# Filling products cut to TensorE's form, a normaliser and key features that read PSUM, and the gate column computed with k and v

## The chip, the cores and the metric

The kernel runs on one core of one Trainium2 chip. A core has five engines with an instruction queue each: TensorE (PE: matrix products from SBUF into PSUM; its weight loads are listed as PEld), VectorE (DVE), ScalarE (ACT), GpSimd (POOL) and SyncE (SP), which here issues all DMAs. Each engine takes its instructions in the order in which they were written; between engines there are semaphores. PSUM has eight banks of 512 float32 columns on 128 partitions.

The metric is the device time of one execution, in microseconds; a change is judged by the median of several runs.

## The reference

Two branches read the same input `x` (2048 positions, 512 features), and a gate mixes them. Branch A is attention with 32 heads of 16 dimensions and one shared key and value head; branch B is a gated MLP whose second half is mixed over the positions.

```python
g = _sigmoid((x * gate_w).sum(-1, keepdims=True))
# A: 32 heads share k and v
q = (x @ wq).reshape(B, S, H, Dh); k = x @ wk; v = x @ wv
scores = jnp.einsum('bhqd,bkd->bhqk', q, k) * Dh ** (-0.5)
o = jnp.einsum('bhqk,bkd->bhqd', softmax(scores), v)
a = o.reshape(B, S, H * Dh) @ wo
# B
z = gelu(jnp.einsum('bsd,df->bsf', x, w_in))
z1, z2 = z[..., :Fh], layernorm(z[..., Fh:])
gg = jnp.einsum('ts,bsf->btf', w_sp, z2) + b_sp[None, :, None]
b = jnp.einsum('bsf,fd->bsd', z1 * gg, w_out)
return g * a + (1 - g) * b
```

S = 2048, D = 512, H = 32, Dh = 16, Fh = 688. Arrays are bfloat16; products sum in float32.

## The kernel before

**Attention without scores.** The scores are small, so the kernel takes exp as a polynomial of the third degree. Then numerator and denominator of the softmax are polynomials in q, whose coefficients are sums ("moments") over all keys: products of k's components times v. A guard checks the bound on the scores; where it fails, a general path runs (not taken here).

**Early stage (0 to about 35 us).** `x` is loaded in four quarters and transposed on TensorE (`g_x`). `g_kv(c)` computes k and v of a quarter (L675, 16 small products), VectorE copies v (L679) and k times 0.25 (L682) from PSUM to SBUF, and then VectorE or GpSimd, whichever the planner finds free, forms products of k's components from the SBUF copy: `inside` (L688, five operations; L684 is the helper's line, L689 the last copy), `across` (L693), `phi` (L698) and `rkv` (L701). `moments` sums them over the keys on TensorE, `moments_out` turns the sums into weights T3, T2b, M2 and so on.

**z2, z1, Q.** The MLP's input products and their gelu: `g_z2` (128 x 344, whole array), `g_z1` (five groups of 128 columns and one, `half5`, cut into four strips), and the q projections (`g_q`).

**Units (59 to 274 us).** 16 units, one for 8 heads' worth of rows (`G`) and a quarter of the queries (`tg`): linear forms of q (L818, squared on ScalarE), four "W" products (L849) into banks 0 to 3, which VectorE (L860) and ScalarE plus GpSimd (L864, L865) multiply by copies Y of q, and sums over them (L871 and L867 to L869). Banks 0 to 3 hold one W group or one group of squares at a time.

**The normaliser**, once for each `tg` (`g_den`, L878): four small strip products give the denominators in PSUM; VectorE adds a constant (L885), takes the reciprocal (L886), multiplies by the gate's part `Er` (L887), all in SBUF float32 (`Rf`), and splits the result into a bfloat16 and its remainder (L891, L892, `Rh`). TensorE spreads `Rh` over the rows (L897, "Rr"), VectorE multiplies the numerators by it (L898).

**Filling work.** The mixing over positions (`g_sp`: 17 products for each of 5 whole groups and one strip group, four times), and the output (`g_out`: 4 + 6 products for each of 16 tiles). The weights of the mixing are loaded by transposing DMAs.

**The gate.** A strided DMA puts `gate_w` into column 32 of `wkvg` (L1040); `g_gate` forms x times gate_w along the columns (strip products), `g_gs` the same along the rows (64 products of one column, L772); both go through exp after the last gelu (L779).

**Who sets the order.** A planner (`Plan.run`) simulates the engines with the costs given in `add` and writes each engine's order; the chip keeps that order. A task has a priority (`pri`, lower first). On TensorE a task knows its *form*: whole array, four column strips, two halves of the rows (W), or four quarters of the rows (squares). Where a task's form differs from the one that TensorE stands in, its priority is worse by 2 and 100 ns are charged. In the kernel before, the form of a product is fixed: `mm1` (L593) is whole, `mmq` (L598) and `half5` (L927) are strips. A group of products opens a PSUM bank and closes it when all its readers ("evac") are done.

Of the kernel before, what the change touches and what calls it, by code (L numbers as in the profile page):

```python
# [16 lines left out]
S = 2048  # L17
# [31 lines left out]
SWITCH = 100.0  # L49
# [5 lines left out]
LAZY = 12  # L55

# [237 lines left out]
class Plan:  # L294
# [8 lines left out]
    def add(self, eng, cost, fn, r=(), w=(), pri=50.0, grp=None, evac=False, dma=0, size=0, chan=None, rate=DMA_RATE, tag="", after=(), opens=(), hold=(), slack=0.0, swp=SWITCH_PRI):  # L303
# [6 lines left out]
        t.tiles = getattr(fn, "tiles", 1)  # L310
# [33 lines left out]
    def run(self, prog, allowed):  # L344
# [6 lines left out]
        tiles = 1  # L351
# [43 lines left out]
        while done < len(self.tasks):  # L395
# [25 lines left out]
            for rt, t in cand[e]:  # L421
# [12 lines left out]
                k = (t.pri + (t.swp if e == "pe" and t.tiles != tiles else 0.0), t.idx)  # L434
# [48 lines left out]
def build_kernel(nc, x_d, wq_d, wk_d, wv_d, wo_d, win_d, wsp_d, bsp_d, wout_d, gw_d, out_d):  # L483
    es = ExitStack()
    with es:
# [24 lines left out]
        gwr = sb("gwr", [128, 4, 32], B16)  # L510
        wo = sb("wo", [128, 4, D], B16)
# [31 lines left out]
        Rf = sb("Rf", [128, 2, 128], F32)  # L543
# [51 lines left out]
        def mmq(b, n, off, lhsTs, rhss, start, stop):  # L595

            def f(t):
                return [t.matmul(ps[32 * q:32 * q + 32, 512 * b() + off:512 * b() + off + n], lhsTs[q], rhss[q],  # L598
                                 start=start, stop=stop, tile_position=(0, 32 * q)) for q in range(4)]
            f.tiles = 4  # L600
            return f
# [46 lines left out]
        add("pool", 1600.0, lambda g: g.memset(psi, 0.0), w=[("psi", c) for c in range(4)], pri=-1)  # L648
# [22 lines left out]
        def g_kv(c):  # L671
            g = Group("any")
            for k in range(4):
                for dt in range(4):
                    add("pe", 26.0, mm1(lambda g=g: g.b, 32, 64 * k, xT[:, dt, 512 * c + 128 * k:512 * c + 128 * k + 128], wkvg[:, dt, 0:32], dt == 0, dt == 3),  # L675
                        r=["wk", "wv", ("x", c, dt)], grp=g, pri=0, tag="kv")
# [5 lines left out]
            add("dve", 130.0, lambda v: v.tensor_scalar(kx[:, t4, :], src()[:, :, 0:16], 0.25, None, ALU.mult), w=[("rk", c)], grp=g, evac=True, pri=0, tag="rk")  # L682
            kq = kx[:, t4, :].rearrange("p k (g i) -> p k g i", i=4)
            mul = lambda v, lo, n, a, b, i: v.tensor_tensor(psi[:, t4, lo:lo + n].rearrange("p k (g i) -> p k g i", i=i), a, b, ALU.mult)  # L684

            def inside(v):

                out = [mul(v, 0, 16, kq, kq, 4), mul(v, 16, 12, kq[:, :, :, 0:3], kq[:, :, :, 1:4], 3), mul(v, 28, 8, kq[:, :, :, 0:2], kq[:, :, :, 2:4], 2),  # L688
                       mul(v, 36, 4, kq[:, :, :, 0:1], kq[:, :, :, 3:4], 1), v.tensor_copy(psi[:, t4, 56:64], kx[:, t4, 0:8])]  # L689
# [626 lines left out]
```

## Time and profile before

| | us |
|---|---|
| median of 3 runs | 300.37 (300.25 to 300.68) |
| the profiled execution | 300.82 |
| its span, first to last instruction | 299.0 |

| engine | instructions | larger groups (us) |
|---|---|---|
| TensorE | 2406 products, 2406 weight loads | mixing 87.3, W 39.2, output 26.3 and 17.1, z2 21.1, sums 20.7 |
| VectorE | 313 | L860 81.8 |
| ScalarE | 232 | L864 71.3, L822 31.1 |
| GpSimd | 96 | L865 136.2 |

The mean granted clock of TensorE is 0.984 of full speed. A row of a group of instructions reads: line, engine, operation, output<-inputs, shape, count, then busy time, mean duration in ns, and the idle time of the engine ahead of it with what ended it. A row of the timeline reads: start, length, engine, line, operation, count. On TensorE the numbers ahead of the shape are rows\*columns of the array. A row of the windows reads: stretch, length, then busy time (and count) of TensorE, weight loads, VectorE, ScalarE, GpSimd, then granted clock, DMA share, GB/s. A row of the waits reads: who, at which line, for whom: total us, times, the longest.

### The profile page before, as it was taken

Reading aid. Unit: us, or ns where it says so; the run is one execution under the profiler, and the core shown is the slowest. Engines: PE = TensorE matmul, PEld = TensorE weight load, DVE = VectorE, ACT = ScalarE, POOL = GpSimd, SP = SyncE. Lnnn points to the kernel's source line nnn. Section 1 sums busy time; section 2 is a strip of 40 time slices with the busy share of each in tenths; the row PEclk is TensorE's granted clock in tenths of the full one; section 3 lists DMA queues with packets and bytes.
Section 4 is the critical chain, followed back from the end, with each engine's and each line's share of the span. In section 5 each row is a group of like instructions: output and inputs, shape, how many; then the busy total and the mean of one; then the engine's idle time right before and its main releaser. Section 6 shows DMA issues by size and latency. Waiting matters only on the chain.

```text
span 299.0 us, 6100 instructions
## 1 busy us (share of the span) xinstructions
PE 279.7 (94%) x2406; PEld 116.1 (39%) x2406; DVE 185.3 (62%) x313; ACT 171.8 (57%) x232; POOL 160.3 (54%) x96
## 2 busy tenths in 40 slices
PE   7897999999999999999997999999969999988992
PEld 3575654444443333332341334233334333233440
DVE  1799996073756796464559586634696734797102
ACT  3484887779884645678571646576324467642001
POOL 8673121055758474674955274957470957775200
PEclk9999999999999999999999899999997999999998
DMA  7938774203786969879960505596932063300002
GB/s 185 347 122 210 166 142 99 44 1 106 213 249 112 208 134 187 165 181 174 168 171 8 142 25 152 107 242 172 158 100 80 0 169 100 106 1 0 3 0 75
DMA packets 51530, 37.56 MB, mean 126 GB/s; under 512 B 36548, under 2 KB 47144, under 8 KB 51496
## 3 DMA queue, kind: packets, MB, share of 16 engines
q1 hardware_dynamic: 51496, 37.12, 54.2%
q8 instruction: 20, 0.33, 0.5%
q14 instruction: 14, 0.11, 0.1%
HBM read 24.52 MB, written 4.19 MB: 96 GB/s over the span
## 4 chain that ended last, share of the span: by engine, by line
PE 72%; DVE 15%; DMA 4%; ACT 2%; SPq 2%; issue 2%; POOL 1%; DVEq 0%; POOLq 0%
PE ps L593 50%; PE ps L849 9%; PE ps L598 9%; DVE Pr L860 3%; DMA X<-qe 2%; DVE Rh L892 2%; PE ps L927 2%; DMA wkvg<-in_A_wv_dram 2%; PE ps L818 2%; DVE wT L684 2%; POOL Pr L865 1%; DVE Rf L887 1%; DVE Pr L698 1%; ACT Wt L864 1%; DVE Rh L891 1%
## 5 line engine op out<-in xcount | busy, mean ns | idle before, releaser
L865 POOL TENSOR_TENSOR Pr<-Wt,Y 128x1024 bf16<-128x1024 bf16 x64 | 136.2, 2129 | 93.8 <-ACT Wt L864 76.0
L860 DVE SCALAR_TENSOR_TENSOR Pr<-ps,T1c,Y 128x1024 bf16<-128x1024 f32 x64 | 81.8, 1278 | 64.0 <-PE ps L849 63.6
L864 ACT ACTIVATE Wt<-ps,T1c 128x1024 bf16<-128x1024 f32 x64 | 71.3, 1115 | 59.1 <-PE ps L849 58.9
L593 PE MATMUL ps<-wT,z 128*128 128x512 bf16 x320 | 87.3, 388 | 0.0
L593 PEld LDWEIGHTS ps<-wT,z 128*128 128x128 bf16 x320 | 28.5, 99 | 44.4 <-issue 20.3
L822 ACT ACTIVATE X<-ps 128x1024 bf16<-128x1024 f32 x32 | 31.1, 1022 | 17.6 <-PE ps L818 17.6
L849 PE MATMUL ps<-X,T 64*128 64x512 bf16 x256 | 39.2, 385 | 1.8 <-DVE Pr L860 1.5
L593 PE MATMUL ps<-wout,z 128*128 128x512 bf16 x96 | 26.3, 381 | 0.8 <-DVE z L966 0.8
L966 DVE TENSOR_TENSOR z<-ps,z 128x512 bf16<-128x512 f32 x20 | 13.7, 686 | 18.1 <-PE ps L593 18.0
L593 PE MATMUL ps<-win,xT 128*128 128x344 bf16 x128 | 21.1, 309 | 0.2
L598 PE MATMUL ps<-Pr,cs 128*32 128x512 bf16 x256 | 20.7, 390 | 0.0
L908 ACT ACTIVATE z<-ps 128x344 bf16<-128x344 f32 x32 | 14.2, 461 | 8.9 <-PE ps L593 6.9
L849 PEld LDWEIGHTS ps<-X,T 64*128 64x128 bf16 x256 | 7.3, 94 | 26.7 <-DVE Pr L860 13.7
L593 PE MATMUL ps<-xT,win 128*128 128x512 bf16 x80 | 17.4, 379 | 0.0
L593 PE MATMUL ps<-wo,win 128*128 128x512 bf16 x64 | 17.1, 380 | 0.0
L992 ACT ACTIVATE outsb<-ps,G 128x512 bf16<-128x512 f32 x14 | 9.6, 689 | 13.0 <-PE ps L593 12.6
L593 PE MATMUL ps<-xT,wq 128*128 128x512 bf16 x64 | 17.0, 379 | 0.1
L898 DVE SCALAR_TENSOR_TENSOR win<-Ns,S,ps 128x512 bf16<-128x512 f32 x16 | 11.7, 741 | 8.5 <-PE ps L593 4.5
L873 ACT ACTIVATE Ns<-ps 128x512 f32<-128x512 f32 x16 | 9.5, 596 | 10.7 <-PE ps L598 10.7
L915 POOL TENSOR_TENSOR rstd<-ve,nhalf 128x4 f32<-128x4 f32 x4 | 4.4, 1092 | 18.6 <-DVE ve L914 18.6
L910 DVE BATCH_NORM_STATS2 bst<-z 128x6 f32<-128x344 bf16 x32 | 14.3, 489 | 0.0
L593 PEld LDWEIGHTS ps<-win,xT 128*128 128x128 bf16 x128 | 11.6, 97 | 5.8 <-issue 0.5
(132 smaller groups left out, 298.9 us busy)
## 6 DMA issues: line engine op xcount, KB each, us to landing
Y<-qe SPq DMA_DIRECT2D x32, 512.0 KB, 4.9
wT<-in_A_x_dram SPq DMA_DIRECT2D x4, 512.0 KB, 5.9
qe<-Qt SPq DMA_DIRECT2D x64, 32.0 KB
out_dram<-outsb SPq DMA_DIRECT2D x16, 128.0 KB, 2.4
X<-qe SPq DMA_DIRECT2D x32, 32.0 KB
Pr<-c_third SPq DMA_DIRECT2D x1, 784.0 KB, 7.9
win<-in_B_w_in_dram SPq DMA_DIRECT2D x2, 344.0 KB, 5.5
win<-in_B_w_in_dram SPq DMA_DIRECT2D x1, 688.0 KB, 8.7
```

What stands on the lines that cost most here:

```text
L593: return lambda t: t.matmul(bank(b(), n, off), lhsT, rhs, start=start, stop=stop)
L598: return [t.matmul(ps[32 * q:32 * q + 32, 512 * b() + off:512 * b() + off + n], lhsTs[q], rhss[q], start=start, stop=stop, tile_position=( ...
L822: add("act", 1030.0, lambda a, h=h: a.activation(X[:, ub, 2 * h:2 * h + 2, :], bank(g.b + 2 * h, 1024).rearrange("p (j n) -> p j n", j=2), ...
L849: return [p.matmul(bank(gw.b + 2 * i + e), T3[64 * e:64 * e + 64, t, :], X[64 * e:64 * e + 64, ub, 2 * h + i, :], start=True, stop=True, t ...
L860: add("dve", 1290.0, lambda v, wv=wv, pi=pi, yv=yv, t=t: v.scalar_tensor_tensor(Pr[:, pi, :, :], wv(), T1c[:, t:t + 1], yv, ALU.add, ALU.m ...
L864: add("act", 1040.0, lambda a, wv=wv, wi=wi, t=t: a.activation(Wt[:, wi, :, :], wv(), ACT.Identity, bias=T1c[:, t:t + 1]), r=["T1c"], w=[( ...
L865: add("pool", 2130.0, lambda v, wi=wi, pi=pi, yv=yv: v.tensor_tensor(Pr[:, pi, :, :], Wt[:, wi, :, :], yv, ALU.mult), r=[("Y", yb, h), ("W ...
L898: add("dve", 750.0, lambda v, gr=gr, u=u, G=G: v.scalar_tensor_tensor(OT[:, tg % 2, G, :], Ns[:, u % NNS, :], S0[:, 0:1], bank(gr.b), ALU. ...
L908: add("act", 456.0, lambda a, g=g, h=h: a.activation(z2[:, FH * st + 344 * h:FH * st + 344 * h + 344], bank(g.b, 344), ACT.Gelu_apprx_tanh ...
L910: add("dve", 495.0, lambda v, h=h: v.bn_stats(bst[:, st, h, :], z2[:, FH * st + 344 * h:FH * st + 344 * h + 344]), r=[("z2", st, h)], w=[( ...
L966: add("dve", 690.0, lambda v: v.tensor_tensor(dst, bank(g.b), dst, ALU.mult), w=[("z1", ft, tc)], grp=g, evac=True, pri=3.5, tag="u")
L992: ea = (620.0, lambda a: a.activation(outsb[:, k, :], bank(g.b), ACT.Copy, scale=G1[:, t2:t2 + 1]))
```

## The change

- **Forms as bits.** Whole, strips, halves and quarters become bits. A new kind of product, `mmx`, is FLEX: whole or strips. If TensorE stands whole, it is issued whole; in strips, or in a form of the rows, it is issued as four strip products of 32 columns each. Q, T2b, Rr, z1 (five groups), the mixing with its bias, and the output become `mmx`. The x transposes, k and v, the moments, z2 and the guard's flag stay whole.

```diff
+        def mmx(b, n, off, lhsT, rhs, start, stop):
+            def f(t):
+                raise AssertionError("no cut chosen")
+            whole = mm1(b, n, off, lhsT, rhs, start, stop)
+            f.cut = {WHOLE: whole, COLS: mmq(b, n, off, [lhsT[:, 32 * q:32 * q + 32] for q in range(4)], [rhs] * 4, start, stop)}
+            f.tiles = FLEX
+            return f
...
-                if t.tiles != tiles:
+                if not t.tiles & tiles:
                     cost += SWITCH
-                tiles = t.tiles
+                    tiles = t.tiles if t.tiles != FLEX else COLS
+                elif t.tiles != FLEX:
+                    tiles = t.tiles
+                if t.tiles == FLEX:
+                    fn = fn.cut[tiles]
```

The planner's charge for a change of form goes from 100 to 110 ns.

- **Normaliser.** One fused operation reads the denominators from PSUM and `Er`; its reciprocal is written into free columns of the same PSUM bank, and the split reads it there. `Er` now holds exp of minus the gate's sum, limited on both sides.

```diff
-            R0, R1 = Rf[:, 0, :], Rf[:, 1, :]
-            add("dve", 280.0, lambda v: v.tensor_scalar(R0, bank(g.b, 128), S * C0, None, ALU.add), w=["R0"], grp=g, evac=True, pri=3, tag="R")
-            add("dve", 1100.0, lambda v: v.reciprocal(R1, R0), r=["R0"], w=["R1"], pri=3, tag="R")
-            add("dve", 290.0, lambda v: v.tensor_tensor(R0, R1, Er[:, 128 * tg:128 * tg + 128], ALU.mult), r=["R1", "Er"], w=["R0"], pri=3, tag="R")
+            R0 = lambda rows=slice(0, 128): ps[rows, 512 * g.b + 128:512 * g.b + 256]
+            add("dve", 290.0, lambda v: v.scalar_tensor_tensor(Rf[:], bank(g.b, 128), S * C0, Er[:, 128 * tg:128 * tg + 128], ALU.add, ALU.mult), r=["Er"], w=["R1"], grp=g, evac=True, pri=3, tag="R")
+            add("dve", 950.0, lambda v: v.reciprocal(R0(), Rf[:]), r=["R1"], w=["R0"], grp=g, evac=True, pri=3, tag="R")
...
-                add("dve", 290.0, lambda v, z=z, a=a, b=b: v.tensor_tensor(Rh[b, z, :], R0[a, :], Rh[a, z, :], ALU.subtract), ...
+                add("dve", 220.0, lambda v, z=z, a=a, b=b: v.tensor_tensor(Rh[b, z, :], R0(a), Rh[a, z, :], ALU.subtract), ..., grp=g, evac=True, pri=3, tag="R")
```

- **Key features.** `inside` and `across` are VectorE's always; `phi` is GpSimd's for quarters 0 and 1 and VectorE's for 2 and 3; `rkv` is GpSimd's always. On VectorE one input (k or v) is read from the PSUM bank of `g_kv`, which stays open until then; GpSimd reads SBUF as before. `across` no longer waits for `inside`. The factor 0.25 goes from the copy of k to the weights: a VectorE operation scales `wk` in place when it has landed.

```diff
-            add({"dve": (950.0, inside), "pool": (2300.0, inside)}, 0, None, r=[("rk", c)], w=[("psi", c)], pri=1, tag="psi")
-            add({"dve": (350.0, across), "pool": (800.0, across)}, 0, None, r=[("rk", c), ("psi", c)], w=[("psx", c)], pri=0.5, tag="psi")
+            ev = dict(grp=g, evac=True)
+            add("dve", 950.0, inside, r=[("rk", c)], w=[("psi", c)], pri=1, tag="psi", **ev)
+            add("dve", 350.0, across, r=[("rk", c)], w=[("psx", c)], pri=0.5, tag="psi", **ev)
```

- **Gate column.** `gate_w` is loaded as one row of 1 KB (`gwl`) right behind wv; four products with a single row turn it into column 32 of `wkvg`, and VectorE copies it there. `g_kv` multiplies by 33 columns in place of 32, so the row sums of the gate come with k and v; `g_gs` with its 64 products is gone, and so is the strided load.

```diff
-                    add("pe", 26.0, mm1(lambda g=g: g.b, 32, 64 * k, xT[...], wkvg[:, dt, 0:32], dt == 0, dt == 3),
-                        r=["wk", "wv", ("x", c, dt)], grp=g, pri=0, tag="kv")
+                    add("pe", 26.0, mm1(lambda g=g: g.b, 33, 64 * k, xT[...], wkvg[:, dt, 0:33], dt == 0, dt == 3),
+                        r=["wk", "wv", "gw", ("x", c, dt)], grp=g, pri=0, tag="kv")
+            add("dve", 80.0, lambda v: v.tensor_scalar(gs[:, t4], src()[:, :, 32], E_MAX, None, ALU.min), w=[("gs", c)], grp=g, evac=True, pri=2.9, tag="gate")
...
+        gw4 = Group("any")
+        for dt in range(4):
+            add("pe", 40.0, mm1(lambda: gw4.b, 1, dt, gwl[:, 128 * dt:128 * dt + 128], ones[0:1, 0:1], True, True), r=["gwl", "ones"], grp=gw4, pri=-0.5, tag="gate")
+        add("dve", 80.0, lambda v: v.tensor_copy(wkvg[:, :, 32:33], bank(gw4.b, 4).unsqueeze(2)), w=["gw"], grp=gw4, evac=True, pri=-0.5, tag="gate")
+        add("pool", 300.0, lambda g: g.tensor_copy(gwr[:], wkvg[:, :, 32:33].broadcast_to([128, 4, 32])), r=["gw"], w=["gwr"], pri=12, tag="gate", slack=20000.0)
```

- **Order.** The first quarter of `x` is loaded ahead of the identity, and z1's last quarter of positions gets priority 14.8 in place of 9.8, behind the first W products (10):

```diff
-                    r=["win1", ("win2", 0), ("x", tc, dt)], grp=g, pri=9.8 + 0.01 * ft, tag="z1")
+                    r=["win1", ("win2", 0), ("x", tc, dt)], grp=g, pri=(9.8 if tc < 3 else 14.8) + 0.01 * ft, tag="z1")
```

More of the change, by code (lines that the diff above doesn't have):

```diff
@@ L48 @@
 DMA_ISSUE = 300.0
-SWITCH = 100.0
+SWITCH = 110.0
 YPRI = 2.1
@@ L309, in add @@
         t.users, t.op, t.eng = [], None, None
-        t.tiles = getattr(fn, "tiles", 1)
+        t.tiles = getattr(fn, "tiles", WHOLE)
         r, w = list(r), list(w)
@@ L350, in run @@
         pipe = [0.0]
-        tiles = 1
+        tiles = WHOLE
         busy = {e: 0.0 for e in ENG}
@@ L433, in run @@
                     continue
-                k = (t.pri + (t.swp if e == "pe" and t.tiles != tiles else 0.0), t.idx)
+                k = (t.pri + (t.swp if e == "pe" and not t.tiles & tiles else 0.0), t.idx)
                 if best is None or k < best[0]:
@@ L638, in build_kernel @@
         load("sp", lambda q: q.dma_start(wkvg[:, :, 0:16], wk_d.rearrange("(dt p) d -> p dt d", p=128)), ["wk"], size=16384, pri=0)
+        add("dve", 80.0, lambda v: v.tensor_scalar(wkvg[:, :, 0:16], wkvg[:, :, 0:16], 0.25, None, ALU.mult), r=["wk"], w=["wk"], pri=-1, tag="wk")
         load("sp", lambda q: q.dma_start(wkvg[:, :, 16:32], wv_d.rearrange("(dt p) d -> p dt d", p=128)), ["wv"], size=16384, pri=0)
+        load("sp", lambda q: q.dma_start(gwl[:], gw_d.rearrange("(one n) -> one n", one=1)), ["gwl"], size=1024, pri=0)
         ld_x(1)
@@ new lines, in inside @@
+                if v is nc.gpsimd:
+                    return out + [v.tensor_copy(psi[:, t4, 56:64], kx[:, t4, 0:8])]
+                return out + [v.tensor_copy(psi[:, t4, 56:64], kp()[:, :, 0:8])]
+            def across(v):
+                up, dn = lambda a: a.unsqueeze(3).broadcast_to([128, 4, 4, 4]), lambda a: a.unsqueeze(2).broadcast_to([128, 4, 4, 4])
+                return [mul(v, psi[:, t4, 64 + 16 * h:80 + 16 * h].rearrange("p k (g i) -> p k g i", i=4), up(kx[:, t4, 8 * h:8 * h + 4]), dn(kx[:, t4, 8 * h + 4:8 * h + 8]),
+                            lambda h=h: up(kp()[:, :, 8 * h:8 * h + 4])) for h in range(2)]
@@ L818, in forms @@
                 return [p.matmul(bank(g.b + j), xe[32 * j:32 * j + 32, :], Qt[32 * j:32 * j + 32, s, :], start=True, stop=True, tile_position=(32 * j, 0)) for j in range(4)]
-            forms.tiles = 3
+            forms.tiles = ROWS32
             add("pe", c_mm(512), forms, r=["cs", ("Q", s)], grp=g, pri=9, tag="sq")
@@ L1039, in build_kernel @@
                             g_z1(ft, tc)
-                    load("sp", nonc(lambda q: q.dma_start(wkvg[:, :, 32:33], gw_d.rearrange("(dt p one) -> p dt one", p=128, one=1))), ["gw"], size=16384, pri=20, hold=[yld[0]])
-                    add("dve", 100.0, lambda v: v.tensor_copy(gwr[:], wkvg[:, :, 32:33].broadcast_to([128, 4, 32])), r=["gw"], w=["gwr"], pri=20, tag="gate")
                     for c in range(4):
                         g_gate(c)
-                    for st in range(NST):
-                        g_gs(st)
                     gate_out()
```

79 lines of the change are left out of this document (41 added, 38 removed).

## The prediction

> **What bounds the kernel now.** I read the page first (its busy times and its chain), then the timeline of TensorE, then the tiles of the normaliser.
>
> ```profile
> span 299.0 us, 6100 instructions
> PE 279.7 (94%) x2406; PEld 116.1 (39%) x2406; DVE 185.3 (62%) x313; ACT 171.8 (57%) x232; POOL 160.3 (54%) x96
> PE 72%; DVE 15%; DMA 4%; ACT 2%; SPq 2%; issue 2%; POOL 1%; DVEq 0%; POOLq 0%
> ```
>
> TensorE is busy 94% of the span and is 72% of the chain that ended last; no other engine is above 62%. But its busy time hides the starts: a row's duration overlaps the next. So I take start-to-start steps from its timeline (start, length, operation, number of matmuls).
>
> ```profile
> 151.16 1.03 PE L593 MATMUL ps<-xT,wq 128*128 128x512 bf16 x4
> 152.02 0.38 PE L593 MATMUL ps<-wT,z 128*128 128x512 bf16 x1
> 152.33 0.73 PE L927 MATMUL ps<-wT,z 128*32 128x256 bf16 x20
> 152.99 0.61 PE L849 MATMUL ps<-X,T 64*128 64x512 bf16 x4
> 153.53 0.40 PE L598 MATMUL ps<-Pr,cs 128*32 128x512 bf16 x4
> 153.76 0.40 PE L598 MATMUL ps<-Prd,cs 128*32 128x128 bf16 x16
> 153.98 0.39 PE L598 MATMUL ps<-Pr,cs 128*32 128x512 bf16 x4
> 154.19 0.23 PE L598 MATMUL ps<-Q,cs 128*32 128x128 bf16 x4
> ```
>
> 128\*128 is the whole array, 128\*32 one of four column strips, 64\*128 a half of the rows. Four whole products take 152.02 - 151.16 = 0.86 us, **0.215 us each**. The next one has 152.33 - 152.02 = 0.31 us, because the form changes behind it: **0.095 us of drain**. The first step after a change is also longer (153.53 to 153.76 is 0.23 us, the same kind of quad later, 153.98 to 154.19, 0.21 us): 0.01 us more. A change of form costs 0.105 us. And a quad of four strips with 512 columns takes 0.21 us, the same as one whole product; five quads of 256 columns take 152.99 - 152.33 = 0.66 us with the drain in it, 0.11 us each. Cut into strips, a product costs TensorE nothing more.
>
> From 59 us, where the units begin, to 281 us the timeline has 259 changes of form. 156 lie on either side of a product with a part of the rows (L849, L818); **103 lie between whole and strip form**. The first and the last of these:
>
> ```profile
> 63.81 0.24 PE L598 MATMUL ps<-Q,cs 128*32 128x128 bf16 x4
> 64.09 1.04 PE L593 MATMUL ps<-xT,wq 128*128 128x512 bf16 x4
> ...
> 279.59 0.61 PE L598 MATMUL ps<-Pr,cs 128*32 128x512 bf16 x8
> 280.14 0.39 PE L593 MATMUL ps<-wT,z 128*128 128x512 bf16 x1
> ```
>
> The second loss is the normaliser (count, then shortest, median and longest ns; below it VectorE, GpSimd and TensorE at the second group of units):
>
> ```profile
> L885 DVE TENSOR_SCALAR Rf<-ps x4: 277/285/292, 98.9 to 262.7; 128x128 f32<-128x128 f32 x4
> L886 DVE RECIPROCAL Rf<-Rf x4: 941/953/953, 99.3 to 263.0; 128x128 f32<-128x128 f32 x4
> L887 DVE TENSOR_TENSOR Rf<-Rf,Er x4: 280/1724/2244, 101.4 to 265.2; 128x128 f32<-128x128 f32 x4
> L891 DVE CAST Rh<-Rf x8: 218/224/1545, 103.1 to 267.7; 64x128 bf16<-64x128 f32 x8
> L892 DVE TENSOR_TENSOR Rh<-Rf,Rh x8: 284/288/2235, 103.6 to 268.3; 64x128 bf16<-64x128 f32 x8
> 159.99 2.55 DVE L892 TENSOR_TENSOR Rh<-Rf,Rh 64x128 bf16<-64x128 f32 x2
> 160.27 2.12 POOL L865 TENSOR_TENSOR Pr<-Wt,Y 128x1024 bf16<-128x1024 bf16 x1 [0.97 <-ACT Wt L864]
> 162.59 0.28 PE L593 MATMUL ps<-Rh,sg 128*128 128x128 bf16 x2 [1.65 <-DVE Rh L892]
> ```
>
> An operation of 0.28 us took 2.24 us: it started 0.03 us after GpSimd's multiply and ended with it. L885, which reads PSUM, never does that. TensorE, which issues in a fixed order, stood behind it with filling work in its queue:
>
> ```profile
> PE ps L593 <- DVE Rh L892: 3.2, 3, 1.7
> PE ps L818 <- DVE Pr L860: 2.3, 1, 2.3
> PE ps L849 <- DVE Pr L860: 1.5, 3, 0.6
> 160.00:180.00 20.00, 18.02 (x138) 6.53 (x139) 15.38 (x17) 9.11 (x11) 10.61 (x5) 0.91 0.23 63
> 220.00:240.00 20.00, 17.65 (x172) 7.46 (x161) 15.05 (x18) 8.37 (x9) 10.49 (x6) 0.91 0.24 64
> ```
>
> These three waits are 3.2 + 2.3 + 1.5 = 7.0 us, nearly all around the four normalisers, where Pr (L860) queues behind them on VectorE. Right after two of the stalls the granted clock is 0.91 over 20 us (third number from the right), 1.00 elsewhere: 0.09 x 20 = 1.8 us twice, 3.6 us. Together **10.6 us**.
>
> **The change part by part.**
>
> *Cut products.* Whole-only products (x transposes, k/v, moments, z2) are over before the units, but for the flag's. From the first strip quad on, every z1, Q, T2b, mixing, Rr and output product may be cut, and the planner cuts it once TensorE stands in strips or in rows. So the 103 changes go: 103 x 0.105 = **-10.8 us**. The 156 at the row forms stay: W and the squares share banks 0 to 3, so each of these 80 groups is entered and left by itself (four of the changes come before 59 us). About 656 products are cut (320 mixing, 96 and 64 output, 20 bias, 16 T2b, 64 Rr, 56 Q, 20 z1), four matmuls for one. What the trace doesn't show is four strips reading the *same* 512 columns; L927's quads read theirs in pairs, at full pace. Bounds: 0 from that row, and 0.07 us a product if three more matmuls were paid as small ones are:
>
> ```profile
> 71.60 0.52 PE L593 MATMUL ps<-wkvg,xT 128*128 128x1 bf16 x15
> 72.04 0.24 PE L598 MATMUL ps<-Q,cs 128*32 128x128 bf16 x4
> ```
>
> 0.44 - 0.10 of drain = 0.34 us for 15, 0.023 us each. I take 0, the row of the same form.
>
> The Trainium skill (TensorEngine Tiling, Instruction Overhead, and Gotcha 2: Feature Incompatibilities) speaks against this part: it gives each matmul some 60 cycles of overhead, and says that column tiling rules out the fast weight load. By that the three extra matmuls would cost 3 x 25 ns x 656 = 49 us (an estimate from that page) and the sum would end near 328 us; the trace's strip quads at 0.21 us disagree.
>
> *Normaliser.* Before: 285 + 953 + 1724 + 2 x 224 + 2 x 288 = 3.99 us of medians, and up to 2.2 us for whichever operation GpSimd catches. After: one fused operation from PSUM and Er, reciprocal into PSUM, two casts and two subtractions with one PSUM input each. Nearest rows, beside L885 and L886:
>
> ```profile
> L679 DVE CAST wT<-ps 128x128 bf16<-128x128 f32 x4 | 1.1, 280 | 1.8 <-PE ps L593 1.8
> L730 DVE TENSOR_TENSOR mT<-ps,mT 128x49 bf16<-128x49 f32 x1 | 0.2, 209 | 0.0
> ```
>
> 0.28 + 0.95 + 2 x 0.28 + 2 x 0.28 = 2.4 us, and nothing to be caught by. The casts get 0.06 us slower; that is in the sum. The planner had charged 280 + 1100 + 290 + 2 x 220 + 2 x 290 = 2.7 us, so TensorE's order fits an unblocked chain, and now that chain runs. Bounds 0 to 10.6 us. I take 85%, **-9.0 us**: some of L860's lateness is W's own. The den bank is held 2 us longer, four times; two banks for filling remain.
>
> *Gate column.* 64 one-column products go:
>
> ```profile
> L593 PE MATMUL ps<-wkvg,xT 128*128 128x1 bf16 x64 | 2.5, 164 | 0.0
> ```
>
> 64 x 0.023 = **-1.5 us**; column 33 rides along with 32 others. Its DMA moves from behind the first units' loads to the front of SP's queue, behind wk and wv and ahead of x's second quarter, which is issued one DMA later; k/v, the first work behind it on TensorE, then waits for one more load, four small products and a copy.
>
> *Early stage.* The same trap is in the key features:
>
> ```profile
> L684 DVE TENSOR_TENSOR wT<-wT 128x64 bf16<-128x64 bf16 (+3 forms) x20 | 5.2, 318 | 0.0
> L689 DVE COPY wT<-wT 128x32 bf16<-128x32 bf16 x4 | 2.4, 594 | 0.0
> 25.77 0.18 PE L593 MATMUL ps<-wT,Pr 128*128 128x17 bf16 x1 [1.57 <-DVE Pr L698]
> ```
>
> VectorE gets 24 + 4 small operations from PSUM, about 0.2 us each (L730's row) and overlapping, in place of 7.6 us; rkv leaves it. TensorE's 1.57 us wait should mostly go. Against it: k/v about 1 us later (one SP issue, products, a copy), and banks held until the features are read. The new scale of wk blocks VectorE until wk lands; behind it is nothing that can start earlier. Bounds -3 to +2; I take **-1.2 us**. z1's last quarter moves behind the first W, from before the units into them: they start its 20 x 0.215 + 4 x 0.11 = 4.7 us earlier and get 4.7 us more of fill, net 0. x ahead of ident on SP's queue: 0, since the transposes need both.
>
> *New waits.* The faster TensorE reaches loads sooner:
>
> ```profile
> L598 PE MATMUL ps<-X,T3d 128*32 128x512 bf16 x64 | 6.1, 385 | 0.5 <-DMA X<-qe 0.5
> ```
>
> 0.5 us now. I put **+1.5 us** (0 to 6).
>
> Sum: 299.0 - 10.8 - 9.0 - 1.5 - 1.2 + 1.5 = 278.0 us of span. The profiled execution took 300.8, 1.8 us around its span: 279.8. It is 0.45 us above the median, 300.37: **279.3 us**, and I say 279.0.
>
> **The rivals.** (1) *The wait moves.* Banks 0 to 3 pass from W to W:
>
> ```profile
> 243.73 0.61 PE L849 MATMUL ps<-X,T 64*128 64x512 bf16 x4
> 246.00 0.60 PE L849 MATMUL ps<-X,T 64*128 64x512 bf16 x4
> ```
>
> 2.27 us undisturbed. 64 W and 16 squares at 2.27 us are 182 us, from 55 to 237 us; at 2.6 us, 263 us. TensorE's own work would end near 294 - 21 = 273 us, so this doesn't bind by itself; but loads or a W late by real durations can: half the normaliser's gain (4.5 us) and 3 us more gone gives 279 + 7 = 286 us. (2) *All the waits go*: 1.6 us more of the normaliser, 1.8 us more of the early stage, no new wait: 279 - 1.6 - 1.8 - 1.5 = 274 us. The low end of the range lies 3 us below that, for small waits of the units that I can't price one by one. (3) *Slower: the cut is dear*. If four strips on one set of columns pay 0.07 us each product: 279 + 656 x 0.07 = 325 us. It decides from 21 / 656 = 0.033 us a product. Against it L927's pairs at 0.11 us. (4) *The changes don't go*, because planned orders keep TensorE whole: 279 + 11 = 290 us; only the flag product could restore that form, so hardly.
>
> **How the numbers follow.** Forecast (275 to 283 us) 0.60; rival 1 (283 to 290) 0.20; rival 2 (below 275) 0.12; rival 3 0.05; rival 4 0.03. Leaving out most of rivals 3 and 4 and the edges of 1 and 2, the range is 271 to 288. A measurement here tells 0.2% (0.6 us) from none. Rival 3 alone can be slower, and only beyond its turning point: slower 0.05, same 0.02, faster 0.93.
>
> **What would show it.** Right: in the timeline from the units on, mixing, Q and output rows read 128\*32, stepping 0.21 us for four; about 156 changes of form; every normaliser operation under 1 us; no clock below 1.00 in the units; no 128x1 products. Wrong: a strip quad stepping above 0.22 us (rival 3); TensorE waiting for X, Pr or wT (rival 1); the first W much later than 55 us.

## The result, and the profile after

| | before | after |
|---|---|---|
| median (us) | 300.31 (299.93 to 300.68, 4 runs) | 281.29 (280.62 to 281.90, 4 runs) |
| the profiled execution | 300.82 | 281.90 |
| its span | 299.0 | 280.1 |
| mean granted clock | 0.984 | 0.997 |

The ratio is 0.9366 (95% interval 0.9341 to 0.9391): 19.0 us faster, 2.3 us above the forecast of 279.0 and inside its range. The ratios here and below leave out runs over 1.5% above their kernel's quickest, which are four of the ten runs of one kernel (the cut alone).

The page of the changed kernel: span, busy time (share) and instructions by engine, and the chain that ended last.

```profile
span 280.1 us, 10009 instructions
PE 263.9 (94%) x4356; PEld 121.0 (43%) x4359; DVE 173.3 (62%) x318; ACT 170.8 (61%) x231; POOL 159.2 (57%) x93
PE 78%; DMA 8%; DVE 5%; ACT 4%; SPq 2%; issue 1%; DVEq 0%; ACTq 0%
```

TensorE is as full as before, 94%, of a shorter span. VectorE's share of the chain fell from 15% to 5%, and that of the DMAs rose from 4% to 8%: a first sign that a wait has moved.

TensorE's timeline in a unit (start, length, operation, matmuls; four matmuls make one quad of strips):

```profile
206.57 0.40 PE L608 MATMUL ps<-wT,z 128*32 128x512 bf16 x4
206.79 0.39 PE L608 MATMUL ps<-bspz,ones 128*32 128x512 bf16 x4
207.01 2.12 PE L608 MATMUL ps<-wT,z 128*32 128x512 bf16 x36
208.95 0.39 PE L608 MATMUL ps<-X,T3d 128*32 128x512 bf16 x4
209.17 0.61 PE L608 MATMUL ps<-Pr,cs 128*32 128x512 bf16 x8
209.71 0.61 PE L877 MATMUL ps<-X,T 64*128 64x512 bf16 x4
```

The mixing reads 128\*32. Its 36 matmuls are nine quads: (208.95 - 207.01) / 9 = **0.216 us a quad**, all four strips on the same 512 columns. That was the price the trace of before couldn't show, and it is nothing: a whole product took 0.215 us. The Trainium skill's overhead of some 60 cycles a matmul (TensorEngine Tiling, Instruction Overhead), by which the prediction had estimated 328 us, isn't paid here. Into the W product (L877, 64\*128) the step is 209.71 - 209.17 = 0.54 us for two quads, 0.11 us more than 2 x 0.216: changes to the row forms cost what they did.

The tiles of the normaliser (shortest, median, longest ns):

```profile
L915 DVE SCALAR_TENSOR_TENSOR Rf<-ps,Er x4: 277/285/292, 89.9 to 245.1; 128x128 f32<-128x128 f32 x4
L916 DVE RECIPROCAL ps<-Rf x4: 961/961/962, 90.2 to 245.4; 128x128 f32<-128x128 f32 x4
```

```profile
L920 DVE CAST Rh<-ps x8: 273/288/295, 91.2 to 248.0; 64x128 bf16<-64x128 f32 x8
L921 DVE TENSOR_TENSOR Rh<-ps,Rh x8: 284/289/294, 91.8 to 248.6; 64x128 bf16<-64x128 f32 x8
```

The operation that before took between 0.284 and 2.235 us (L892) now takes between 0.284 and 0.294. The sum is 0.285 + 0.961 + 2 x 0.288 + 2 x 0.289 = 2.4 us, as worked out.

The windows of after over the two stretches where the granted clock was 0.91 (third number from the right):

```profile
160.00:180.00 20.00, 18.75 (x334) 8.28 (x331) 14.54 (x21) 10.82 (x12) 13.58 (x7) 1.00 0.33 87
220.00:240.00 20.00, 20.00 (x354) 8.55 (x349) 9.63 (x10) 13.69 (x16) 12.76 (x6) 1.00 0.50 131
```

The waits of after, where TensorE is the one that waits (total us, times, longest):

```profile
PE ps L877 <- DVE Pr L888: 4.1, 5, 1.1
PE ps L608 <- DMA X<-qe: 2.9, 3, 1.5
```

`Rh` is gone from the list (3.2 us before). W (L877) on Pr went from 1.5 to 4.1 us, and X from 0.5 to 2.9 us.

To set steps against terms I add up TensorE's timeline: from each product's start to the next one's I take off its pace (0.216 us for 512 columns, less in proportion), then up to 0.106 us at a change of form; a rest above 0.06 us is a wait, and smaller ones count with the products. What lies at a lower granted clock has its own row.

| us of TensorE's time | before | after | difference | predicted |
|---|---|---|---|---|
| changes between whole and strips | 10.7 (103) | 0 | -10.7 | -10.8 |
| changes to and from row forms | 15.5 (160) | 16.2 (160) | +0.7 | 0 |
| lower clock | 3.6 | 0 | -3.6 | -3.6, of the normaliser's -9.0 |
| waits of the early stage (to 59 us, to 54 us) | 7.1 | 4.3 | -2.8 | -1.2 |
| waits from there on | 11.6 | 11.2 | **-0.4** | -5.4 (the rest of -9.0) + 1.5 |
| products at their pace | 244.1 | 241.8 | -2.3 | -1.5 |
| sum | 292.7 | 273.4 | -19.3 | -21.0 |

Five rows came within 2 us. The fifth didn't: the old waits of the units went, and nearly as many new ones came.

### The profile page after: what moved, and what is told of

Read it like the earlier page. It is cut to its first block, busy times and chain, and to the rows that moved or that the text cites. A ratio compares the mean times of both kernels' runs of the same rounds, so it can differ in the third digit from the quotient of the medians.

```text
span 280.1 us, 10009 instructions
## 1 busy us (share of the span) xinstructions
PE 263.9 (94%) x4356; PEld 121.0 (43%) x4359; DVE 173.3 (62%) x318; ACT 170.8 (61%) x231; POOL 159.2 (57%) x93
## 4 chain that ended last, share of the span: by engine, by line
PE 78%; DMA 8%; DVE 5%; ACT 4%; SPq 2%; issue 1%; DVEq 0%; ACTq 0%
PE ps L608 51%; PE ps L603 12%; PE ps L877 10%; DMA X<-qe 6%; PE ps L956 3%; DVE Pr L888 2%; DMA wT<-in_A_x_dram 2%; PE ps L846 2%; ACT Wt L892 1%; ACT X L850 1%; ACT Q L826 1%; ACT Qt L820 1%; DVE qk L1101 1%; ACT Ns L901 0%; DVE outsb L1022 0%
## 5 line engine op out<-in xcount | busy, mean ns | idle before, releaser
L892 ACT ACTIVATE Wt<-ps,T1c 128x1024 bf16<-128x1024 f32 x64 | 71.4, 1116 | 55.7 <-PE ps L877 55.3
L608 PE MATMUL ps<-wT,z 128*32 128x512 bf16 x1280 | 84.8, 380 | 0.0
L608 PEld LDWEIGHTS ps<-wT,z 128*32 128x32 bf16 x1280 | 32.4, 97 | 35.7 <-issue 8.6
L877 PE MATMUL ps<-X,T 64*128 64x512 bf16 x256 | 38.8, 381 | 4.3 <-DVE Pr L888 4.1
L608 PE MATMUL ps<-wout,z 128*32 128x512 bf16 x384 | 26.8, 380 | 0.5 <-DVE z L998 0.5
L995 DVE TENSOR_TENSOR z<-ps,z 128x512 bf16<-128x512 f32 x20 | 13.7, 687 | 13.8 <-PE ps L608 13.6
L877 PEld LDWEIGHTS ps<-X,T 64*128 64x128 bf16 x256 | 7.3, 94 | 30.0 <-DVE Pr L888 15.7
L608 PE MATMUL ps<-Pr,cs 128*32 128x512 bf16 x256 | 20.0, 381 | 0.0
L608 PE MATMUL ps<-wo,win 128*32 128x512 bf16 x256 | 18.0, 380 | 0.0
L1021 ACT ACTIVATE outsb<-ps,G 128x512 bf16<-128x512 f32 x14 | 9.5, 689 | 13.6 <-PE ps L608 13.6
L902 DVE SCALAR_TENSOR_TENSOR Prd<-ps,T1d,Qt 128x512 bf16<-128x512 f32 x16 | 11.9, 747 | 7.1 <-PE ps L608 6.9
L608 PEld LDWEIGHTS ps<-wout,z 128*32 128x32 bf16 x384 | 9.8, 96 | 11.8 <-issue 2.6
L608 PE MATMUL ps<-xT,wq 128*32 128x512 bf16 x224 | 14.5, 380 | 0.3 <-DVE qm L1049 0.2
L967 ACT ACTIVATE z<-ps 128x512 bf16<-128x512 f32 x20 | 11.8, 599 | 4.5 <-PE ps L608 2.6
```

What stands on the lines that cost most here:

```text
L877: return [p.matmul(bank(gw.b + 2 * i + e), T3[64 * e:64 * e + 64, t, :], X[64 * e:64 * e + 64, ub, 2 * h + i, :], start=True, stop=True, t ...
L892: add("act", 1040.0, lambda a, wv=wv, wi=wi, t=t: a.activation(Wt[:, wi, :, :], wv(), ACT.Identity, bias=T1c[:, t:t + 1]), r=["T1c"], w=[( ...
L902: add("dve", 750.0, lambda v: v.scalar_tensor_tensor(Prd[:, u % NPD, :], bank(gd.b), T1d[:, 0:1], Qt[:, s, :], ALU.add, ALU.mult), r=["T1d ...
L967: add("act", 540.0, lambda a: a.activation(z1[:, ft, 512 * tc:512 * tc + 512], bank(g.b), ACT.Gelu_apprx_tanh), w=[("z1", ft, tc)], grp=g, ...
L995: add("dve", 690.0, lambda v: v.tensor_tensor(dst, bank(g.b), dst, ALU.mult), w=[("z1", ft, tc)], grp=g, evac=True, pri=3.5, tag="u")
```

## The experiments

Each kernel ran in turn with the kernel before on the same chip: 300.22, 300.19 and 300.08 us there in the three sets. The planner's "own end" in an expectation is the end of its simulation, and no measurement.

### Parts undone, in the changed kernel's order

The order of each engine is kept here, so that only the price of one part changes. First the products, all issued whole:

```diff
                 if t.tiles == FLEX:
-                    fn = fn.cut[tiles]
+                    fn = fn.cut[WHOLE]
```

> The changed kernel with its order of work on every engine kept, but each filling product issued whole instead of as four strips. In that order 128 changes between whole and strip form come back (counted in the trace of the changed kernel by giving its filling products the whole form); the changes at row forms stay at 160. My theory (a change costs 0.105 us, a cut product nothing): 281.3 + 128 x 0.105 = 294.7 us, less what lands in TensorE's waits (10 us of waits are there, so perhaps 2 us): 292 to 295 us. Rival (most of the gain came from the new order, the drains were hidden by waits): under 285 us.

Measured: **290.17 us** (289.76 to 290.35), ratio 0.9675 (0.9634 to 0.9716). The page's chain:

```profile
PE 90%; DVE 4%; ACT 1%; DMA 1%; SPq 1%; issue 1%; DVEq 0%; ACTq 0%
```

By the addition above, 130 changes between whole and strips cost 13.6 us, but waits fell from 15.5 to 9.4 us; the DMA's share of the chain fell from 8% to 1%. So 8.9 us is what the cut is worth at the end, less than the 11 to 14 expected: it takes out 13.6 and gets some 6 back as waits, not 2. A TensorE that is slower everywhere meets the same loads later.

Then the split of the normaliser from SBUF again, with a copy of the reciprocal in a tile of its own:

```diff
+        Rs = sb("Rs", [128, 128], F32)
...
-            R0 = lambda rows=slice(0, 128): ps[rows, 512 * g.b + 128:512 * g.b + 256]
+            R0 = lambda rows=slice(0, 128): Rs[rows, :]
```

> The changed kernel with its order kept; the reciprocal is written to an SBUF tile, and the casts and subtractions of the normaliser read it there (single-input casts, subtractions with two SBUF inputs). The same number of operations. My theory (operations that read two SBUF inputs, or cast from SBUF, are stopped by GpSimd's multiply): some of the 16 operations take 1 to 2.2 us, TensorE stalls behind two or three of the four splits, 2 to 7 us more: 283 to 288 us. Rival (the gain came from two operations fewer and from the planner knowing the length): 281.3 within 0.6 us.

Measured: **288.68 us** (287.67 to 290.97), ratio 0.9649 (0.9586 to 0.9712): 7.4 us, just above the 2 to 7 expected. TensorE's timeline at the last two normalisers:

```profile
203.78 0.41 PE L609 MATMUL ps<-Rh,sg 128*32 128x128 bf16 x16 [3.31 <-DVE Rh L922]
...
251.23 0.30 PE L609 MATMUL ps<-Rh,sg 128*32 128x128 bf16 x8 [1.19 <-DVE Rh L922]
253.36 0.83 PE L609 MATMUL ps<-Rh,sg 128*32 128x128 bf16 x24 [1.83 <-DVE Rh L922]
```

The waits on `Rh` are back (6.3 us, three times) from four operations per normaliser that read SBUF. The timeline of all engines shows the pair at 198.8:

```profile
198.83 2.12 POOL L894 TENSOR_TENSOR Pr<-Wt,Y 128x1024 bf16<-128x1024 bf16 x1 [0.26 <-ACT Wt L893]
198.85 2.43 DVE L921 CAST Rh<-Rs 64x128 bf16<-64x128 f32 x2
```

Two casts that take 0.22 us each without company took 2.43 us together: the first alone took 2.18 and ended 0.08 us behind GpSimd's multiply. The Trainium skill (SBUF — State Buffer, Who interferes with whom) has VectorE and GpSimd share a pair of SBUF ports, and whoever issues first holds it for its whole instruction. It counts a VectorE operation with two SBUF inputs among those that contend, and a cast if it runs in a 2-port mode, but not one that has a single SBUF input outside these modes. The traces agree, though none says in which mode a cast ran: the subtraction took up to 2.235 us with two SBUF inputs (L892 before) and 0.294 with one (L921 after), the cast up to 2.177 us from SBUF here and 0.295 from PSUM.

Third, the key features on VectorE from SBUF:

```diff
-                return e.tensor_tensor(dst, a if e is nc.gpsimd else p(), b, ALU.mult)
+                return e.tensor_tensor(dst, a, b, ALU.mult)
...
-                return out + [v.tensor_copy(psi[:, t4, 56:64], kp()[:, :, 0:8])]
+                return out + [v.tensor_copy(psi[:, t4, 56:64], kx[:, t4, 0:8])]
```

> The changed kernel with its order kept; VectorE's key features read k from SBUF (two SBUF inputs) instead of PSUM. My theory of the early stage: single features are stopped by GpSimd's rkv and phi for up to 1.9 us, the moments end 2 to 4 us later, and since TensorE has z2 and z1 to do meanwhile, 0.5 to 2.5 us reach the end: 282 to 284 us. Rival (the early stage is hidden behind z2 and z1): 281.3 within 0.6 us.

Measured: **285.49 us** (284.76 to 285.82), ratio 0.9511 (0.9467 to 0.9554); 4.2 us against 1 to 3 expected. Its timeline of TensorE in the early stage, where from 10.5 to 36 us the same view of the changed kernel shows no idle time at all:

```profile
16.55 0.40 PE L603 MATMUL ps<-ident,wT 128*128 128x128 bf16 x4 [1.52 <-DVE xT L689]
19.46 0.30 PE L603 MATMUL ps<-wT 128*128 128x288 bf16 x1 [0.60 <-DVE wT L720]
28.28 0.18 PE L603 MATMUL ps<-wT,Pr 128*128 128x17 bf16 x1 [0.42 <-DVE Pr L711]
```

VectorE's 24 short features (L711) take 12.0 us here, the longest 1.93, and in the changed kernel 4.7 us, the longest 0.22; the medians are alike, 0.216 and 0.203 us, so reading SBUF isn't dear in itself. TensorE's largest wait is not on a feature, but on the copy of a transpose (`xT`, L689) that VectorE had queued behind the features. The first W came at 52.49 in place of 48.43 us, 4.1 us later, and the end 4.2 us later: nothing behind the early stage takes up a delay there.

### Parts alone, on the kernel before

The cut, in the order of before (strips from the first W on):

```diff
+                units = units or t.tag == "W"
+                if units and hasattr(fn, "strips"):
+                    fn = fn.strips
```

> The kernel before with its order kept on every engine; from the first W on, its filling products are issued as four strips (the cut alone). The normaliser stays in SBUF. Of 103 changes between the two forms about 10 are left, around the one-column gate products and the flag. My theory: 300.3 - 93 x 0.105 = 290.5 us, a little more if the drains lay in stalls: 290 to 292 us. Rival (a cut product with four strips on the same columns is dearer): slower than 291 by 656 times what a quad takes above 0.216 us.

Measured: **297.99 us** (294.47 to 300.58, 10 runs), ratio 0.990 (0.9855 to 0.9946): by the ratio 3.0 us (1.6 to 4.4), where 9 were expected. The waits of its profiled run, one of the two quickest (294.81 us):

```profile
PE ps L601 <- DVE Rh L900: 5.1, 4, 1.8
PE ps L857 <- DVE Pr L868: 4.6, 5, 3.0
```

There changes between whole and strips fell from 10.7 to 1.0 us, but waits rose from 18.7 to 22.9: a TensorE that is early waits for the old normaliser all the longer. That run is 5.4 us below the median of before, so there these waits account for what the cut didn't pay; what the longer runs lost besides, no trace shows.

The changed normaliser alone, planned anew: the edits of the section on the change, and with them

```diff
-            ... Er[:], bank(gG.b), E_MAX, None, ALU.min)
+            ... Er[:], bank(gG.b), E_MAX, -E_MAX, ALU.min, ALU.max)
...
-            ... a.activation(Er[:], Er[:], ACT.Exp)
+            ... a.activation(Er[:], Er[:], ACT.Exp, scale=-1.0)
```

> The kernel before with the changed normaliser alone (two operations fewer, PSUM operands, its bank held until the split is done); the planner orders the work anew. My theory (GpSimd stopped the normaliser, TensorE stood behind it, and its clock fell after two of the stalls): the clock stays at 1.00, no normaliser operation is over 1 us, the waits for Rh are gone: about 300.2 - 8 = 292 us. Rival (the drains and the bank hold eat it): above 297 us.

Measured: **291.85 us** (291.64 to 292.32), ratio 0.9711 (0.9649 to 0.9773). Waits fell from 18.7 to 12.8 us, and the granted clock stays at 1 in the units. 8.3 us from this part, with the order planned anew. Then the cut of the first experiment of this section, in that same order:

> The same order as in the run before it (kernel before with the changed normaliser alone), with the filling products issued as four strips from the first W on: both large parts together, without the key features, the gate column and the new order. My theory now (the cut saves about 93 x 0.105 = 10 us of drains, and loses some of it only where TensorE then stands behind something else): 7 to 10 us less than that run, 282 to 286 us. Rival (the cut alone gave only 2 us, so it gives 2 us here as well): 289 us or more.

Measured: **284.04 us** (283.51 to 285.17), ratio 0.9449 (0.9383 to 0.9515). On top of the normaliser the same cut is worth 7.8 us, not 3.

The gate column alone, beside k and v, planned anew:

```diff
-                    add("pe", 26.0, mm1(..., 32, ..., wkvg[:, dt, 0:32], ...
+                    add("pe", 26.0, mm1(..., 33, ..., wkvg[:, dt, 0:33], ...
...
-                    for st in range(NST):
-                        g_gs(st)
```

> The kernel before with the gate column beside k and v alone (the 64 one-column products gone, the filling and the normaliser as before). The prediction's third term is -1.5 us, most of it TensorE time that goes from the quarter stage: about 299 us against 300.2 on the same chip, between 298 and 301. Rival: the column's removal moves the order of the work enough to change which normaliser operations collide with GpSimd, and the time moves by more than 2 us either way (below 298 or above 302).

Measured: **305.87 us** (305.17 to 306.31), ratio 1.0205 (1.0178 to 1.0233): slower than before, by the rival's way. Its products at their pace take 242.6 us against 244.1, the -1.5 expected. But its waits list, and two rows of its timeline of TensorE:

```profile
PE ps L594 <- DVE Rh L894: 8.4, 4, 3.1
```

```profile
105.62 0.52 PE L594 MATMUL ps<-Rh,sg 128*128 128x128 bf16 x4 [3.08 <-DVE Rh L894]
107.16 0.91 PE L851 MATMUL ps<-X,T 64*128 64x512 bf16 x4 [1.03 <-DVE Pr L862]
```

`Rh` costs 8.4 us in place of 3.2, and the lower clock 5.5 in place of 3.6; W on Pr, 2.5 us here, is no smaller than the 1.5 before. The normaliser's operations are those of before, and as many of them are stopped by a GpSimd multiply: six take over 1.5 us in either kernel, 11.6 us in sum before and 13.0 here. What moved is the order around them (already the first W comes at 40.65 us in place of 59.65, the second at 59.27 in place of 61.72), and with it how long TensorE stands behind each stop. So the 5.8 us are the price of one new order, and not of the column's own work.

### The waits that came

In the changed kernel TensorE stands at 74.40 us (start, length, operation, matmuls, idle time ahead and what ended it):

```profile
68.49 0.40 PE L608 MATMUL ps<-Qt,T2b 128*32 128x512 bf16 x4
69.17 1.05 PE L608 MATMUL ps<-xT,win 128*32 128x512 bf16 x16 [0.28 <-ACT Q L826]
70.27 0.61 PE L877 MATMUL ps<-X,T 64*128 64x512 bf16 x4
...
72.33 0.61 PE L877 MATMUL ps<-X,T 64*128 64x512 bf16 x4 [0.41 <-DVE Pr L888]
72.86 0.40 PE L608 MATMUL ps<-xT,win 128*32 128x512 bf16 x4
73.09 0.23 PE L608 MATMUL ps<-Q,cs 128*32 128x128 bf16 x4
74.40 0.40 PE L608 MATMUL ps<-X,T3d 128*32 128x512 bf16 x4 [1.08 <-DMA X<-qe]
```

The D group gives the denominators. Its first product (T2b) needs only Q and opens a PSUM bank at 68.49; its second (T3d) needs a load of X, at 74.40. For 5.9 us one of the few banks for filling holds a group that can't go on. My reading is that filling work that has no bank can't be put ahead of the waits. The repair is one argument: the planner opens that bank only once X is due.

```diff
-                    add("pe", c_mm(512), mmx(..., T2b[:], Qt[:, s, :], True, False), ..., grp=gd, pri=pr_, tag="D")
+                    add("pe", c_mm(512), mmx(..., T2b[:], Qt[:, s, :], True, False), ..., grp=gd, pri=pr_, tag="D", opens=xr)
```

> The changed kernel with one more rule for the planner: the D group opens its PSUM bank only when the row load of X for its unit is due to have landed, instead of when it has been issued. My theory of the new waits (a D group holds one of three filling banks while it waits for X, so that fill has no bank and W comes late; and a D product put too early stops TensorE behind X): the waits for X, 3.4 us, go and some of the W waits: 277 to 280 us. Rival (the new waits are W's own cycle through banks 0 to 3): 281.3 within 0.8 us.

Measured: **275.56 us** (275.18 to 275.92), ratio 0.9168 (0.911 to 0.9227), 5.7 us faster than the changed kernel and below the 277 to 280 expected. Its timeline of TensorE there:

```profile
67.51 0.61 PE L877 MATMUL ps<-X,T 64*128 64x512 bf16 x4 [0.69 <-DVE Pr L888]
68.05 1.91 PE L608 MATMUL ps<-xT,win 128*32 128x512 bf16 x32
69.89 0.61 PE L877 MATMUL ps<-X,T 64*128 64x512 bf16 x4
...
72.61 0.39 PE L608 MATMUL ps<-Qt,T2b 128*32 128x512 bf16 x4
73.63 0.40 PE L608 MATMUL ps<-X,T3d 128*32 128x512 bf16 x4 [0.64 <-DMA X<-qe]
```

Eight quads of z1 now run without a break at 68.05, T2b comes 1.0 us ahead of T3d in place of 5.9, and X is waited for once (0.6 us) in place of three times (2.9). Waits over the run: 9.6 us against 15.5; W's waits on Pr fell too, from 4.1 to 2.3. The order elsewhere was planned anew too, so that the rule pays is shown, and which of its moves pays most is not.

The same rule in the kernel before:

> The kernel before with one rule more in its planner: the filling group whose first product needs no load but whose later ones need X opens its PSUM bank only once X is due. If a bank held open for X cost the kernel before nothing, since other waits ended last there, 300 us within 1.5. If the held bank was already a loss before the change, as the planner's own end (282.0 against 283.6) has it, about 298; if it was as dear as in the changed kernel (5.7 us there), 295.

Measured: **299.62 us** (298.11 to 301.43, 10 runs), ratio 0.9992 (0.9963 to 1.0021). No change. The first row of its waits:

```profile
PE ps L593 <- DVE Rh L892: 8.5, 3, 3.1
```

X isn't waited for any more (0.5 us before), but the normaliser's waits are 8.5 us in place of 3.2 + 2.3 + 1.5 = 7.0: the collisions moved by more than the rule could win (in the profiled run, 301.20 us, one of the longest of the ten). A bank held open was no loss that shows in the kernel before; in the changed one the rule, with the order that it brings, is worth 5.7 us.

z1's last quarter early again, in the changed kernel:

```diff
-                    ..., pri=(9.8 if tc < 3 else 14.8) + 0.01 * ft, tag="z1")
+                    ..., pri=9.8 + 0.01 * ft, tag="z1")
```

> The changed kernel with the priority of z1's last quarter as before, so that all of z1 goes ahead of the first W; ordered anew. My theory (net nothing: the first W starts 5 us later, and the fill is the same in sum): 281.3 within 1.5 us, first W near 54 us. Rival (the earlier start of the units is what brings the gain): 284 us or more.

Measured: **279.04 us** (278.56 to 280.17), ratio 0.9283 (0.9219 to 0.9348): 2.25 us faster by the medians than with z1 late (the runs lie apart, 280.17 at most against 280.62 at least; the ratios' intervals touch), and its waits are 11.3 us. The first W, expected near 54 us, came at 47.93 (48.43 in the changed kernel); only from the second on do the two part, 58.37 against 55.03. So the priority moved less than its expectation said, and the order that the change brings is by the medians itself a small loss. With the rule for the D bank too:

> The changed kernel with both repairs: the rule that opens the X group's bank late (275.6 alone) and the old, early place of z1 in all quarters (279.0 alone against 281.3). If the two are separate losses, 273.3; if they are the same idle time reached by two ways, 275 to 276; a rival in which the early z1 delays key features that no longer have slack gives 277 or more.

Measured: **276.98 us** (276.33 to 277.39), ratio 0.9242 (0.9219 to 0.9265), 1.4 us *slower* by the medians than with the rule alone (again the runs lie apart and the intervals touch). The losses don't add: with the bank free, late z1 is no loss, and rather the better filling. The third expected case (277 or more) gives nearly this time, but not for its reason: TensorE's waits list of this run names no key feature, and its first W comes at 47.78 us, no later than the 47.99 with the rule alone.

Last, the rule for the D bank with a longer allowance for the linear layers (`SLACK_LIN` 2500 to 3500):

> The changed kernel with the rule that opens the X group's bank late, and the planner's allowance for the linear layers at 3.5 us. The planner's own end falls by 0.4 us (272.8 against 273.2): 275 us if the chip follows the plan, 273 to 277 within what reordering has moved it; a time outside of that says that collisions, and not the plan, set the end.

Measured: **274.77 us** (274.20 to 275.47), ratio 0.9159 (0.9126 to 0.9192). The intervals of the ratios overlap with those of the rule alone, so the allowance is not shown to matter. Both are faster than either kernel of the case, by about 25 us against before.

## Why the prediction was right, and where not

**Cut products, -10.8.** Right on TensorE: -10.7 us, 103 changes gone, a quad at 0.216 us. At the end of the run the cut was worth 8.9 us in place, 7.8 on top of the normaliser, and 3 without it. The prediction added it to the normaliser's gain as if each stood by itself (19.8 us). The two together gave 16.2 us, more than the 3 + 8.3 that they gave alone: a drain saved is paid out only where nothing else ends last.

**Normaliser, -9.0.** Right: 8.3 us alone (planned anew), operations of 2.4 us in all, the clock at 1 in the units. Undoing only its split costs 7.4 us.

**Gate column, -1.5.** Right as TensorE's time (-1.5 alone). In the kernel before the one order tried with it lost 5.8 us, behind the stops of the old normaliser; whether it pays by itself with the new one wasn't run. The load moved to the front costs next to nothing: TensorE waits 0.51 us for it where it had waited 0.61 us for wv, as these rows of the timelines of before and after show.

```profile
8.71 0.23 PE L593 MATMUL ps<-wkvg,xT 128*128 128x32 bf16 x3 [0.61 <-DMA wkvg<-in_A_wv_dram]
```

```profile
8.01 0.25 PE L603 MATMUL ps<-ones,gwl 1*128 1x1 bf16 x4 [0.51 <-DMA gwl<-in_gate_w_dram]
```

**Early stage, -1.2 (bounds -3 to +2).** The mechanism was right and the size wrong. At the second W, which all of z1 but a few strips precedes in both, the kernel before stands at 61.72 us and the kernel with z1 early at 58.37 (rows of their timelines):

```profile
61.72 0.61 PE L849 MATMUL ps<-X,T 64*128 64x512 bf16 x4 [0.27 <-ACT z L940]
```

```profile
58.37 0.60 PE L877 MATMUL ps<-X,T 64*128 64x512 bf16 x4
```

That is 3.3 us, and waits up to that point went from 7.5 to 3.0 us. Against the gain the prediction had set 1 us for later k and v; their first products start at 8.93 us in place of 8.71, 0.2 later. It had priced the features by their own waits, not by the copies of x that queue behind them on VectorE (a wait of 0.8 us before, of 1.52 in the run with features from SBUF, none after). And it had put x ahead of the identity at nothing, since the transposes need both: before, they waited 0.49 us for x and began at 5.70 us, after at 5.08 with no wait. What that did for the end by itself wasn't tried.

**z1 behind the first W, "net 0".** Wrong in the kernel as changed: about 2 us lost; with the D bank free, about 1 us won. The reason given (units start 4.7 us earlier and get 4.7 us more of fill) counted work and left out whether a bank is free for it; and against the kernel with z1 early the first W comes 0.5 us later, the second 3.3 us earlier.

**New waits, +1.5 (0 to 6).** This is the step that failed, by its size. Of 11.6 us of waits behind the early stage 5.4 were to go (the rest of the -9.0), which leaves 6.2; there are 11.2, so 5.0 us are new in place of 1.5. If all 7.0 us of the old ones went, as the lists suggest, 6.6 are new, above the bound. Rival 1 named the kind, loads and W late by real durations, and the waits list shows both. The prediction had priced X by the 0.5 us that it cost then. The waits lists of the runs tell what made it dear: X isn't waited for with the new normaliser alone, nor in the changed kernel with its products whole; it costs 0.8 us with the cut on top of the normaliser, 2.9 in the changed kernel. So the loads had lived on the drains that the cut took out. W's waits on Pr came with the new order: 1.4 us with the normaliser alone, 1.8 with the cut on top, but 3.6 in the changed kernel even with its products whole. Nor had the prediction seen what one repair takes back: the bank that D holds while X is on its way. The terms that gave more than forecast, the early stage above all, made up for part of it; to that extent it is luck that the sum came within 2.3 us.

**The rivals.** A dear cut is excluded (0.216 us a quad). That the changes would not go is excluded too (none left). All waits going, 274 us, is about what the kernel with the repaired D bank reaches, by another road: it still waits for 9.6 us.

## What to carry to other kernels

Stalls and drains in an engine's fixed order cover later losses, so price each part of a change alone and on top of the others before adding them: the same cut was worth 3 or 7.8 us. Where products share a few PSUM banks, look for a group whose first product is early and whose next waits for a load, and open its bank when the load is due: with the order planned anew that was worth 5.7 us in the changed kernel, and nothing in the kernel before. And let VectorE read PSUM where GpSimd streams from SBUF beside it: a subtraction that could take 2.24 us then took 0.29 at most.

## What the runs showed of the hardware

That a GpSimd multiply of 2.12 us holds up a VectorE operation of 0.28 us for its whole length was in the trace of before. Which of the two is held is settled within hundredths of a us. Twice in that trace the multiply is on record 0.01 to 0.03 us ahead of the same operation of the normaliser:

```profile
217.84 0.28 DVE L887 TENSOR_TENSOR Rf<-Rf,Er 128x128 f32<-128x128 f32 x1
217.82 2.28 POOL L865 TENSOR_TENSOR Pr<-Wt,Y 128x1024 bf16<-128x1024 bf16 x1 [0.18 <-ACT Wt L864]
265.21 2.24 DVE L887 TENSOR_TENSOR Rf<-Rf,Er 128x128 f32<-128x128 f32 x1
265.19 2.12 POOL L865 TENSOR_TENSOR Pr<-Wt,Y 128x1024 bf16<-128x1024 bf16 x1 [0.76 <-ACT Wt L864]
```

At 217.84 VectorE's operation took its 0.28 us and the multiply was 0.16 us longer; at 265.21 the operation took 2.24. And much hangs on the order around such pairs: with the old normaliser's instructions unchanged, another order cost 5.8 us (the gate column alone).

When the clock falls can be read from the traces. Each fall in the units lasts 3.41 us at half the clock, and the falls of one trace begin whole multiples of 3.413 us apart: at 163.21 and 224.65 us before (18 times), at 108.35 and 220.99 in the kernel before with the rule for the D bank (33 times). Cut into stretches of that length, the fourteen traces have, from 45 us to the last W, ten that are followed by a fall, and TensorE is idle for 1.6 to 3.0 us in each of them; the 868 others have 1.7 us at most. So in these traces a fall follows a stretch that is idle for about half or more, whether by one wait or by several. In the kernel with the split from SBUF the wait of 3.31 us at 203.78 falls on two stretches and costs nothing, while those of 1.19 and 1.83 us, which end at 251.23 and 253.36, share one. In the kernel before with the rule for the D bank a single wait of 2.80 us, which ends at 220.94, was enough. Windows of the first kernel:

```profile
198.69:202.10 3.41, 1.77 (x28) 0.43 (x16) 3.32 (x5) 1.12 (x2) 2.85 (x2) 1.00 1.03 222
202.10:205.51 3.41, 1.73 (x56) 1.01 (x60) 3.38 (x3) 0.00 (x0) 1.48 (x1) 1.00 0.72 142
205.51:208.92 3.41, 3.41 (x72) 1.31 (x60) 3.36 (x5) 1.11 (x1) 0.73 (x1) 1.00 0.47 147
249.89:253.30 3.41, 0.45 (x12) 0.12 (x8) 3.32 (x4) 0.98 (x1) 2.79 (x2) 1.00 0.00 0
253.30:256.71 3.41, 3.35 (x52) 1.58 (x52) 3.20 (x5) 0.60 (x1) 0.00 (x0) 0.50 0.02 5
```

And of the second:

```profile
217.58:220.99 3.41, 0.61 (x4) 0.12 (x3) 3.28 (x5) 0.96 (x1) 2.63 (x2) 1.00 0.00 0
220.99:224.40 3.41, 3.41 (x17) 1.51 (x21) 3.38 (x6) 0.00 (x0) 0.00 (x0) 0.50 0.04 10
```

The ends of matmuls are modelled in the profile, so the line between 1.6 and 1.7 us is no sharp one, and no run was made to test it.

The clock also makes most of the spread between the runs of that second kernel. Its ten runs go from 298.11 to 301.43 us, with mean granted clocks from 1.000 down to 0.988; less the time that the lower clock took (one minus the clock, times the span), they all lie between 297.6 and 298.5 us. The thirteen runs of the kernel before beside them go from 298.85 to 302.49 us, and less it from 295.3 to 296.8. Where the stretches of 3.413 us lie against the start of the span differs from trace to trace, so that the same stalls may cost a fall in one run and none in the next; that this is the reason is argued, not tested.
